# Packed output projection and moved edge work in a gated attention and expert kernel

## The chip, the cores and the metric

The kernel runs on one core of a Trainium2 chip. Its engines work side by side, each in its own order: TensorE (PE, with its weight loads as PEld), VectorE (DVE), ScalarE (ACT), GpSimd (POOL) and SyncE (SP, which here only issues DMAs). ACT and POOL issue DMAs too. The metric is the time of one execution on the device in microseconds (us). Lower is better.

## What is computed

x has 2048 rows of 448 numbers in float32. Two branches read it, and a gate mixes them:

```python
x = A_x
g = _sigmoid((x * gate_w).sum(-1, keepdims=True))
a = _A_ref(x, A_wqkv, A_wo)
b = _B_ref(x, B_w_gate, B_w1, B_w2)
return g * a + (1 - g) * b
```

Branch a is attention with 16 heads of 28 numbers: softmax(q k^T / sqrt(28)) v for each head, the heads side by side, times wo (448 x 448). Branch b is a mixture of 8 experts: each row goes to the two experts with the largest of 8 logits x @ w_gate, each expert is silu(x @ w1[e]) @ w2[e] with 1792 hidden numbers, and the two results are added with softmax weights of the two logits.

## The kernel before

Most products are made from float32 numbers split in two: a high part h (rounded to the type float32r) and a low part l = value - h. A product is then h*h + h*l + l*h, three matmuls. A 448-row operand is held as four blocks of 128 partitions. The fourth has only 64 rows, so those rows stand in it twice: the upper 64 partitions take the low part (`split_xl`, L162), so that block needs two matmuls, not three. That makes 11 matmuls for a full product.

The stages, in PE's order:

1. **Front and v projection** (L251 to L391). x comes in 16 tiles of 128 rows on SP. `wv_r` holds the v columns of wqkv, and behind them the columns of wgate (D to D + E) and of gate_w (one column): one product gives v, the logits and the gate. `rows4` (L208) loads a 448-row operand in three DMAs: rows 0 to 383, and rows 384 to 447 twice. ACT splits `wv_r` block by block (L351), DVE makes the low parts (L335), and PE does 11 matmuls for a tile (L369). Before that, PE turns identity matrices (`busy`).
2. **q and k projection** (L561 to L617): `qk_tile` does four groups of 11 matmuls (L572), each into one of four PSUM banks `pq`; ACT copies the high part out (`hi`, L581), DVE the low part (`lo`, L584), and SP stores both to DRAM. Between the matmuls (at two places of a group, `A_AT`) `route(5)` issues up to five steps of the generator `routing` (L400); a step that yields a true value ends the call. Its last steps build, for four pairs of halves, one-hot masks `ob` and `ot` on DVE (L495, L499), products of `ot` on POOL and ACT (L502, L504), and then matmuls that turn them into lists of row numbers (L515). The last `qk_tile` also transposes the first expert's five x tiles in its groups (`first_x`, L599; `x_tile`, L227).
3. **Experts** (L785 to L896). For each expert, two halves of 7 hidden tiles: 22 matmuls for a hidden tile (L818) in two accumulators, silu on ACT (L820 to L826), the high part of a w2 block on ACT (L726, called at L823) and its low part on POOL (L732, called at L829), w1's split for the tiles ahead, and the low part of the hidden numbers on POOL (L741). Then five row tiles times w2 (L862 for the short tile k = 4, L868 for the others; the order is 4, 0, 1, 2, 3, counted by n_k). Between these, `worked` fits in matmuls of the row maxima of the scores (L106), which DVE reduces (L125) and SP stores (L144). An expert has room for 576 rows; rows beyond are done by `spilled` (L744), a loop over a count known only at run time. It is entered in the last expert, within the fourth row tile (n_k = 3, k = 2), ahead of f = 3.
4. **Attention** (L970 to L1041). A unit is one of four groups of four heads (g) and one of four quarters of the queries (qc), so there are 16 units (u = 4g + qc), with 16 key tiles (kt) each. Scores run three key tiles ahead of the products with v, which gather in one PSUM bank `po` (L1003). At a unit's end DVE copies `po` to `osb` (L1007) and POOL sends the row sums through DRAM to all partitions (`spread_sums`, L956). In the next unit `divide` (L964) multiplies by the reciprocal, one quarter at each of kt = 6 to 9, into `OT`. `OT`, `wo_h` and `wo_l` hold one 128-partition block for each head group: four heads of 28 rows at partitions 0, 32, 64 and 96, the rest unused. `beside` (L1011) also issues K and V loads, and in the last head group the gathers of the experts' rows (`fetch_routed`, L919, two indirect DMAs on POOL) and their weighted sum (`routed`, L928, two DVE operations).
5. **Output projection** (L1043 to L1051). For each of 16 tiles: `project` (L946), 12 matmuls (three for each of the four blocks) into one of four PSUM banks in turn; `split_o` of the tile four ahead (ACT L939, DVE L943; four buffers); `finish` (L951), which adds the gated sums on DVE and stores the tile on SP. The last unit is divided a quarter at a time behind tiles 3 to 6.

The order on PE, DVE and ACT is the program's in stages 1 and 2; in the experts POOL's too; in attention and after it only PE's and DVE's. The other engines' instructions, SP's always, are placed by the framework's scheduler at compile time.

## Time and profile before

| | us |
|---|---|
| median of 3 runs | 1485.94 |
| lowest and highest of them | 1484.88 and 1489.9 |
| profiled execution | 1484.16 |
| its span, first to last instruction | 1482.4 |
| front and v projection | 0 to 53 |
| q and k projection | 53 to 132.3 |
| experts | 132.3 to 946.6 |
| attention | 946.6 to 1439.3 |
| output projection | 1439.3 to 1482.4 |

The bounds of the stages are the starts of their first matmuls in the trace. A row of the timeline names start, length, engine, line, operation, what is written and read, and a count; the bracket gives the engine's idle time before it and what ended that. A row of the waits names the waiting engine, tile and line, then what it waited for, then the total in us, how often, and the longest. A row of the chain of work that ended last gives start, length and what. A row of the busy times by stage gives the stretch, its length, the busy time of each engine with its number of instructions, the clock that TensorE was granted (1.00 is full), the mean busy share of the DMA engines, and GB/s.

### The profile page before, as it was taken

How to read it: one execution, taken by the hardware profiler on the slowest of the kernel's cores; microseconds unless marked ns; L12 is line 12 of the kernel's file. 1: busy time of each engine (PE TensorE's matmuls, PEld its weight loads, DVE VectorE, ACT ScalarE, POOL GpSimd, SP SyncE). 2: the span in 40 equal slices, each digit the busy share in tenths (PEclk: the TensorE clock that was granted, in tenths of full speed). 3: DMA queues.
4: the chain of work that ended last, by engine and by line, in shares of the span. 5: the costliest groups of instructions: out<-in, count | busy, mean ns of one | idle time of the engine just before them, and what ended most of it. 6: DMA issues, size and time to landing. Idle time of an engine off the chain costs nothing.

```text
span 1482.4 us, 28384 instructions
## 1 busy us (share of the span) xinstructions
PE 1460.7 (99%) x11380; PEld 980.4 (66%) x11380; DVE 786.5 (53%) x680; ACT 902.9 (61%) x1579; POOL 657.5 (44%) x707
## 2 busy tenths in 40 slices
PE   8999999999999999999999999799999999999998
PEld 7878888888878888888788888433333333333348
DVE  4645767767767767777777778011123111223245
ACT  5334355344444543543444434499999999999981
POOL 2123587587566765874775656211122111124330
PEclk9999999999999999999999999999999999999999
DMA  9777631343133323323431320300221221143212
GB/s 323 259 265 226 178 96 55 107 130 117 62 108 115 89 90 110 103 68 99 129 118 39 107 61 4 89 21 22 77 66 44 61 63 33 29 120 98 74 42 99
DMA packets 107958, 147.97 MB, mean 100 GB/s; under 512 B 17356, under 2 KB 83308, under 8 KB 107824
## 3 DMA queue, kind: packets, MB, share of 16 engines
q1 hardware_dynamic: 98192, 124.90, 27.3%
q0 software_dynamic: 9344, 20.78, 4.7%
q8 instruction: 90, 1.47, 0.4%
q10 hardware_dynamic: 288, 0.46, 0.1%
q14 instruction: 44, 0.36, 0.1%
HBM read 108.56 MB, written 37.51 MB: 99 GB/s over the span
## 4 chain that ended last, share of the span: by engine, by line
PE 95%; issue 1%; DVE 1%; ACT 1%; DMA 1%; POOL 0%; SPq 0%; POOLq 0%; ACTq 0%
PE acc L818 23%; PE acc L868 19%; PE po L1003 17%; PE ps L991 16%; PE pm L106 6%; PE pq L572 4%; PE acc L862 3%; PE pq L369 2%; PE ps L949 2%; PE acc L106 2%; PE acc L714 1%; PE po L949 1%; PE pt L331 0%; DMA wv_r<-in_gate_w_dram 0%; DVE ot L499 0%
## 5 line engine op out<-in xcount | busy, mean ns | idle before, releaser
L125 DVE TENSOR_REDUCE mp<-pm 128x6 f32<-128x3072 f32 (+1 forms) x164 | 542.0, 3306 | 121.3 <-PE pm L106 121.3
L994 ACT ACTIVATE P<-ps 128x1536 f32<-128x1536 f32 x256 | 371.4, 1451 | 0.2
L1003 PE MATMUL po<-P,V 128*32 128x512 f32 x2048 | 272.8, 604 | 0.0
L818 PE MATMUL acc<-xeh,w1l 128*128 128x288 f32 x880 | 259.4, 302 | 0.0
L818 PE MATMUL acc<-xeh,w1h 128*128 128x288 f32 x880 | 256.0, 298 | 0.0
L991 PEld LDWEIGHTS ps<-Q,Kh 29*128 29x128 f32 (+1 forms) x2048 | 78.8, 183 | 217.7 <-ACT P L993 212.4
L732 POOL TENSOR_TENSOR w2l<-w2r,w2h 128x448 fp32r<-128x448 f32 x112 | 129.3, 1154 | 198.4 <-ACT w2h L726 198.4
L991 PE MATMUL ps<-Q,Kh 29*128 29x512 f32 (+1 forms) x2048 | 191.4, 444 | 3.7 <-ACT P L993 3.6
L818 PE MATMUL acc<-xel,w1h 128*128 128x288 f32 x660 | 194.8, 295 | 0.0
L958 POOL DMA_DIRECT2D sum_d<-osb x64 | 32.0, 510 | 347.0 <-DVE osb L1007 323.3
L820 ACT ACTIVATE hh<-acc 128x288 fp32r<-128x288 f32 x224 | 92.5, 413 | 148.3 <-PE acc L818 148.1
L818 PEld LDWEIGHTS acc<-xeh,w1l 128*128 128x128 f32 x880 | 165.9, 189 | 21.7 <-issue 21.5
L868 PE MATMUL acc<-w2h,hh 128*128 128x448 f32 x448 | 173.7, 388 | 4.9 <-DMA Kh<-qkh_d 4.9
L818 PEld LDWEIGHTS acc<-xeh,w1h 128*128 128x128 f32 x880 | 165.8, 188 | 7.6 <-issue 7.3
L868 PE MATMUL acc<-w2h,hl 128*128 128x448 f32 x448 | 169.1, 378 | 0.0
L1007 DVE COPY osb<-po 128x512 f32<-128x512 f32 x16 | 11.1, 692 | 293.6 <-PE po L1003 243.6
L868 PE MATMUL acc<-w2l,hh 128*128 128x448 f32 x448 | 164.4, 367 | 0.0
L993 ACT ACTIVATE P<-ps 128x512 f32<-128x512 f32 x256 | 153.5, 600 | 3.5 <-PE ps L991 2.3
L694 POOL TENSOR_TENSOR w1l<-w1r,w1h 128x512 fp32r<-128x512 f32 (+1 forms) x88 | 137.8, 1566 | 18.9 <-ACT w1h L688 6.7
L741 POOL TENSOR_TENSOR hl<-hf,hh 128x512 fp32r<-128x512 f32 x112 | 143.5, 1288 | 0.0
L818 PEld LDWEIGHTS acc<-xel,w1h 128*128 128x128 f32 x660 | 124.6, 189 | 1.7 <-issue 1.5
L106 PE MATMUL pm<-khg,qg 28*128 28x512 f32 x969 | 118.2, 454 | 0.4 <-DVE mp L125 0.4
(183 smaller groups left out, 1963.0 us busy)
## 6 DMA issues: line engine op xcount, KB each, us to landing
w2r<-in_B_w_dram SPq DMA_DIRECT2D x112, 224.0 KB
w1r<-in_B_w_dram SPq DMA_DIRECT2D x56, 384.0 KB
w1r<-in_B_w_dram SPq DMA_DIRECT2D x112, 64.0 KB
qkh_d<-hi SPq DMA_DIRECT2D x28, 256.0 KB
qkl_d<-lo SPq DMA_DIRECT2D x28, 256.0 KB
ys_d<-yo SPq DMA_DIRECT2D x32, 224.0 KB
ys_d<-zf SPq DMA_DIRECT2D x24, 224.0 KB
v_d<-v_s SPq DMA_DIRECT2D x16, 256.0 KB
```

The costliest lines, as they stand in the source:

```text
L106: nc.tensor.matmul(banks[n], qgs[g, qt // 4][rw, (qt % 4) * 128:(qt % 4 + 1) * 128], kh[g, kc][rw], start=True, stop=True)
L125: nc.vector.tensor_reduce(mp[:, (o + lo) % 256:(o + lo) % 256 + hi - lo], pm[:, lo:hi], axis=AX.X, op=ALU.max)
L694: nc.gpsimd.tensor_tensor(l[:, :, half], r[:, :, half], h[:, :, half].bitcast(F32), op=ALU.subtract)
L732: nc.gpsimd.tensor_tensor(w2l, w2r, w2h.bitcast(F32), op=ALU.subtract)
L741: nc.gpsimd.tensor_tensor(hl, hf32, hh[:, 0:512].bitcast(F32), op=ALU.subtract)
L818: nc.tensor.matmul(pu[:, 0:HC], a, b[:, cs], start=i == 0, stop=i == len(mms) - 1)
L820: nc.scalar.activation(hh[:, cs], pu[:, 0:HC], AF.Silu)
L868: nc.tensor.matmul(py[:n, 0:w], a[:, cs], b, start=i == 0, stop=i == 3 * NH - 1)
L991: nc.tensor.matmul(p3[:, j - 1] if j else p1, k[rw, ks], qs[u][rw, c], start=i == 0, stop=i == 2)
L993: nc.scalar.activation(P[:, 0], p1, AF.Exp, scale=SCALE)
L994: nc.scalar.activation(P[:, 1:4], p3, AF.Exp, scale=SCALE)
L1003: nc.tensor.matmul(po[32 * j:32 * j + 32], v[:, kt % 8, 32 * j:32 * j + 32], P[:, j], start=kt == 0, stop=kt == NT - 1)
```

## The change

- **Front**: wgate's rows 0 to 383 are loaded on ACT's queue, between the two wv blocks there, and its last rows, twice, on SP's, after wv's last and ahead of x tile 2. Before, all three were on POOL's queue ahead of gate_w's last rows.
- **Routing**: the step that makes `ob` now ends its call of `route`; one of the pauses behind the pairs is gone.
- **First x tiles**: they are transposed two, two, one, none in the groups of the last `qk_tile`; before: two, one, one, one.
- **w2**: in the first half of the first expert, w2's blocks are split one hidden tile later; the last hidden tile there splits two.
- **Overflow loop**: it is entered ahead of f = 6, the last one of the row tile, and not of f = 3.
- **Output projection**: `wo` and `OT` are packed as the other 448-row operands are, in four blocks of 128 with the last 64 rows twice, so a tile takes 11 matmuls. `divide` works in place on `osb`; once its last quarter is done, SP copies each head's rows to their place in `OT`, in pieces where a head crosses a block's edge, and twice for rows from 384 on. The last unit's four quarters are all divided behind tile 3.
- **Gathers**: each unit u fetches tile u at kt = 1 and sums it at kt = 12.

```diff
@@ -254,8 +254,9 @@
         nc.gpsimd.memset(warm, 0.0)
         load_x(0)
         load_x(1)
-        for b in range(2):
-            nc.scalar.dma_start(wv_r[:, b, 0:D], wqkv[b * 128:(b + 1) * 128, 2 * D:3 * D])
+        nc.scalar.dma_start(wv_r[:, 0, 0:D], wqkv[0:128, 2 * D:3 * D])
+        rows4(wv_r[:, :, D:D + E], wgate, nc.scalar, slice(0, 1))
+        nc.scalar.dma_start(wv_r[:, 1, 0:D], wqkv[128:256, 2 * D:3 * D])
         nc.scalar.activation(warm[:, 1:2], warm[:, 0:1], AF.Copy)
         nc.sync.dma_start(wv_r[:, 2, 0:D], wqkv[256:384, 2 * D:3 * D])
         for b in range(2):
@@ -264,8 +265,8 @@
         nc.gpsimd.iota(jp, pattern=[[1, 128]], base=0, channel_multiplier=-1,
                        allow_small_or_imprecise_dtypes=True)
         nc.vector.tensor_scalar(ident, jp, 0.0, None, op0=ALU.is_equal)
-        rows4(wv_r[:, :, D:D + E], wgate, nc.gpsimd)
         rows4(wv_r[:, :, D + E:D + E + 1], gw.unsqueeze(1), nc.gpsimd, slice(1, 3))
+        rows4(wv_r[:, :, D:D + E], wgate, nc.sync, slice(1, 3))
         nc.gpsimd.memset(wv_r[:, :, NV - 1], 0.0)
         for t in range(2, NXT - 1):
             load_x(t)
@@ -494,7 +495,7 @@
                     ob = wk.tile([128, 8, 128], BF, name="xt", bufs=NXT)
                     nc.vector.tensor_tensor(ob, bc(iob.unsqueeze(1), [128, 8, 128]),
                                             bc(bb[:, c, hs_].unsqueeze(2), [128, 8, 128]), op=ALU.is_equal)
-                    yield
+                    yield "pause"
                     ot = sb.tile([128, 8, NTL], BF, name="ot", bufs=2)
                     nc.vector.tensor_tensor(ot, bc(iob[:, 0:NTL].unsqueeze(1), [128, 8, NTL]),
                                             bc(tb[:, c, hs_].unsqueeze(2), [128, 8, NTL]), op=ALU.is_equal)
@@ -504,7 +505,6 @@
                     nc.scalar.mul(mv[:, :, 1], ot, iop)
                     pairs.append((ob, mv))
                     yield "pause"
-            yield "pause"
             yield "pause"
             yield "pause"
             yield "pause"
@@ -597,7 +597,7 @@
         xe = []
 
         def first_x(c):
-            for k in ((0, 1), (2,), (3,), (4,))[c]:
+            for k in ((0, 1), (2, 3), (4,), ())[c]:
                 x_tile(xgs[k], k, lambda: ps.tile([128, 4, 128], F32, name="pt"), *xe)
 
         next(ms)
@@ -798,6 +798,8 @@
                     p = e * NP + ft // 2
                     i2 = e * NF + ft
 
+                    w2_now = [i2] if e or hf else [i2 - 1, i2][f == 0:1 + (f == NH - 1)]
+
                     ahead = p + 1 if 2 <= ft < 6 or ft >= 8 and ft < 12 or e == 0 and ft < 2 else None
                     w1h, w1l = w1t[p][1:]
                     fs = HALVES[ft % 2]
@@ -820,13 +822,15 @@
                         nc.scalar.activation(hh[:, cs], pu[:, 0:HC], AF.Silu)
                         if c == 0:
                             nc.scalar.activation(hf32[:, 0:HC], pu[:, 0:HC], AF.Silu)
-                            split_w2_high(i2)
+                            for i in w2_now:
+                                split_w2_high(i)
                         else:
                             nc.scalar.activation(hf32[:, HC:512], pu[:, 0:512 - HC], AF.Silu)
                             nc.scalar.activation(ht, pu[:, 512 - HC:HC], AF.Silu)
                             if ahead:
                                 split_w1_high(ahead, HALVES[ft % 2])
-                    split_w2_low(i2)
+                    for i in w2_now:
+                        split_w2_low(i)
                     if ahead:
                         split_w1_low(ahead, HALVES[ft % 2])
                     if lag:
@@ -854,7 +858,7 @@
                     for f in range(NH):
                         hh, hl, ht = hs[f]
                         w2h, w2l, w2r = w2t[base + f]
-                        if (e, hf, n_k, f) == (E - 1, 1, 3, 3):
+                        if (e, hf, n_k, f) == (E - 1, 1, 3, NH - 1):
                             assert not flush and next(ms, 0) == 0
                             spilled()
                         if k == 4:
@@ -903,18 +907,20 @@
     v1[1] = load_v(0, 1)
     sb = ctx.enter_context(tc.tile_pool(name="pc_sb", bufs=2, reuse_waits="tile"))
     ps = ctx.enter_context(tc.tile_pool(name="pc_ps", bufs=1, space=PSUM, reuse_waits="tile"))
-    wo_h = sb.tile([128, NG, D], F32R, name="wo_h", bufs=1)
-    wo_l = sb.tile([128, NG, D], F32R, name="wo_l", bufs=1)
-    OT = sb.tile([128, NG, S], F32, name="OT", bufs=1)
-
-    def split_wo(g):
-        w_ = sb.tile([128, D], F32, name="yg0")
-        nc.gpsimd.memset(w_, 0.0)
-        for j in range(4):
-            r0 = (4 * g + j) * DH
-            nc.gpsimd.dma_start(w_[32 * j:32 * j + DH], wo[r0:r0 + DH])
-        nc.vector.tensor_copy(wo_h[:, g], w_)
-        nc.vector.tensor_tensor(wo_l[:, g], w_, wo_h[:, g].bitcast(F32), op=ALU.subtract)
+
+    wo_h = sb.tile([128, 4, D], F32R, name="wo_h", bufs=1)
+    wo_l = sb.tile([128, 4, D], F32R, name="wo_l", bufs=1)
+    OT = sb.tile([128, 4, S], F32, name="OT", bufs=1)
+
+    def split_wo(b):
+        w_ = sb.tile([128, D], F32, name="wo_r")
+        if b < 3:
+            nc.gpsimd.dma_start(w_, wo[b * 128:(b + 1) * 128])
+        else:
+            nc.gpsimd.dma_start(w_[0:64], wo[384:448])
+            nc.gpsimd.dma_start(w_[64:128], wo[384:448])
+        nc.vector.tensor_copy(wo_h[:, b], w_)
+        nc.vector.tensor_tensor(wo_l[:, b], w_, wo_h[:, b].bitcast(F32), op=ALU.subtract)
 
     def fetch_routed(t):
         yg = []
@@ -934,19 +940,22 @@
 
     def split_o(t, eng):
         ts = slice(t * 128, (t + 1) * 128)
-        oh = sb.tile([128, NG, 128], F32R, name="oh", bufs=4)
+        oh = sb.tile([128, 4, 128], F32R, name="oh", bufs=4)
         if eng is nc.scalar:
             nc.scalar.activation(oh, OT[:, :, ts], AF.Copy)
         else:
             nc.vector.tensor_copy(oh, OT[:, :, ts])
-        ol = sb.tile([128, NG, 128], F32R, name="ol", bufs=4)
-        nc.vector.tensor_tensor(ol, OT[:, :, ts], oh.bitcast(F32), op=ALU.subtract)
+        ol = sb.tile([128, 3, 128], F32R, name="ol", bufs=4)
+        split_xl(OT[:, :, ts], oh, ol, 128)
         halves[t] = (oh, ol)
 
     def project(pa_, oh, ol):
-        for g in range(NG):
-            for i, (a, b) in enumerate(((oh, wo_h), (oh, wo_l), (ol, wo_h))):
-                nc.tensor.matmul(pa_, a[:, g], b[:, g], start=g == 0 and i == 0, stop=g == NG - 1 and i == 2)
+        mms = []
+        for j in range(3):
+            mms += [(oh[:, j], wo_h[:, j]), (oh[:, j], wo_l[:, j]), (ol[:, j], wo_h[:, j])]
+        mms += [(oh[:, 3], wo_h[:, 3]), (oh[:, 3], wo_l[:, 3])]
+        for i, (a, b) in enumerate(mms):
+            nc.tensor.matmul(pa_, a, b, start=i == 0, stop=i == len(mms) - 1)
 
     def finish(t, pa_, b1):
         nc.vector.scalar_tensor_tensor(b1, pa_, coef[:, 0, t:t + 1], b1, op0=ALU.mult, op1=ALU.add)
@@ -964,8 +973,22 @@
     def divide(g, qc, k, osb, rs):
         cs = slice(k * 128, (k + 1) * 128)
         nc.vector.reciprocal(rs[:, cs], rs[:, cs])
-        nc.vector.tensor_tensor(OT[:, g, qc * 512 + k * 128:qc * 512 + (k + 1) * 128], osb[:, cs],
-                                rs[:, cs], op=ALU.mult)
+        nc.vector.tensor_tensor(osb[:, cs], osb[:, cs], rs[:, cs], op=ALU.mult)
+        if k < 3:
+            return
+
+        qs_ = slice(qc * 512, (qc + 1) * 512)
+        for j in range(4):
+            r = (4 * g + j) * DH
+            end = r + DH
+            p = 32 * j
+            while r < end:
+                n = min(end, (r // 128 + 1) * 128) - r
+                for twice in range(2 if r >= 384 else 1):
+                    o = r % 128 + 64 * twice
+                    nc.sync.dma_start(OT[o:o + n, r // 128, qs_], osb[p:p + n])
+                r += n
+                p += n
 
     ctx.enter_context(tc.manual_schedule(engines={mybir.EngineType.PE, mybir.EngineType.DVE}))
     todo = []
@@ -1024,11 +1047,10 @@
             held[g][1][1] = load_v(g, 1)
         if g == 1 and qc == 1 and kt % 4 == 1:
             split_wo(kt // 4)
-        if g == NG - 1 and kt in (1, 4, 7, 10):
-            fetch_routed(4 * qc + kt // 3)
-        if g == NG - 1 and kt in (3, 6, 12, 14):
-            t = 4 * qc + {3: 0, 6: 1, 12: 2, 14: 3}[kt]
-            b1s[t] = routed(t)
+        if kt == 1:
+            fetch_routed(u)
+        if kt == 12:
+            b1s[u] = routed(u)
         if u == 4 * NG - 1 and kt in (2, 5, 11, 13):
             split_o({2: 0, 5: 1, 11: 2, 13: 3}[kt], nc.vector)
 
@@ -1046,8 +1068,9 @@
         project(pa_, *halves.pop(t))
         if t + 4 < NT:
             split_o(t + 4, nc.scalar)
-        if 3 <= t < 7:
-            divide(NG - 1, 3, t - 3, *ended[4 * NG - 1])
+        if t == 3:
+            for k in range(4):
+                divide(NG - 1, 3, k, *ended[4 * NG - 1])
         finish(t, pa_, b1s.pop(t))
```

## The prediction

> **What bounds the kernel now.** I read the page first, then the busy times by stage, then the waits of TensorE over the whole span, and only then the places that those waits name.
>
> ```profile
> span 1482.4 us, 28384 instructions
> PE 1460.7 (99%) x11380; PEld 980.4 (66%) x11380; DVE 786.5 (53%) x680; ACT 902.9 (61%) x1579; POOL 657.5 (44%) x707
> ```
>
> ```profile
> 0.00:53.00 53.00, 48.20 (x256) 43.09 (x257) 23.78 (x60) 26.13 (x61) 11.68 (x59) 1.00 0.93 320
> 53.00:132.30 79.30, 75.59 (x378) 61.36 (x377) 42.17 (x101) 25.27 (x48) 13.77 (x11) 1.00 0.72 245
> 132.30:946.60 814.30, 808.69 (x5440) 669.90 (x5440) 591.53 (x300) 355.98 (x944) 524.12 (x456) 1.00 0.32 96
> 946.60:1439.30 492.70, 488.97 (x5121) 170.06 (x5120) 105.72 (x183) 487.89 (x514) 103.91 (x173) 1.00 0.22 60
> 1439.30:1482.40 43.10, 39.19 (x195) 35.98 (x192) 23.32 (x37) 7.61 (x12) 4.02 (x8) 0.99 0.26 92
> ```
>
> The columns after a window's length are the busy times of PE, PEld, DVE, ACT and POOL. The stages are: v projection and routing logits; q and k projections; experts; attention; output projection. In every one PE is busy nearly throughout. So the time falls in two ways only: PE gets fewer matmuls, or one of its few pauses goes. The pauses, longest first:
>
> ```profile
> PE acc L868 <- DMA Kh<-qkh_d: 4.9, 1, 4.9
> ...
> PE pq L572 <- DVE lo L584: 2.3, 1, 2.3
> PE acc L818 <- DVE xeh L164: 1.4, 1, 1.4
> ...
> PE acc L818 <- ACT ht L826: 0.3, 1, 0.3
> ```
>
> Each row gives total, count and longest. The rows L868, L572 and the two L818 are pauses that this change works on; so is a late start for lack of data, which this list shows only in pieces.
>
> **Part 1, the front.** The first x tile is projected when all four row blocks of wv_r, with the columns of wgate and gw, have landed.
>
> ```profile
> 2.55 1.90 POOL L211 DMA_DIRECT2D wv_r<-in_B_w_gate_dram  x3
> ...
> 4.42 1.07 POOL L211 DMA_DIRECT2D wv_r<-in_gate_w_dram  x2
> 7.91 1.54 ACT L351 ACTIVATE xeh<-wv_r 128x458 fp32r<-128x458 f32 x3 [1.72 <-DMA wv_r<-in_B_w_gate_dram]
> 10.23 0.59 ACT L351 ACTIVATE xeh<-wv_r 128x458 fp32r<-128x458 f32 x1 [0.78 <-DMA wv_r<-in_gate_w_dram]
> 11.54 0.48 PE L369 MATMUL pq<-xel,xh 128*128 128x458 f32 x1 [0.17 <-DVE xel L335]
> ```
>
> The reader is to see one queue: POOL issues three wgate pieces and only then the last two of gw, whose landing at 10.23 us releases the last split; PE goes on at 11.54. With wgate on ACT's and SP's queues, POOL issues gw 1.9 us sooner (the three issues' 1.90 us). The same landing delay then puts the split at about 8.3 us, and ACT, whose first three splits take 1.54 us, is ready by then if the wgate piece lands before 6.9 us. It is issued at about 1.2 us on ACT, behind one block of wv. On SP the two wgate pieces delay the x loads by two issues, about 1.1 us as POOL's two at 4.42; only tile 2's could matter, which is needed after the last split. I take 1.8 us. Bounds: 0, if the many small pieces on ACT's queue hold up wv's second block by as much; 2.5, if gw isn't last any more (7.91 + 1.54 - 1.72 = 7.7 us in place of 10.23).
>
> **Part 2, routing.** The reader is to see a chain that goes round between DVE and ACT, in program order on both.
>
> ```profile
> 72.34 0.69 DVE L584 TENSOR_TENSOR lo<-pq,hi 128x512 fp32r<-128x512 f32 x1 [1.28 <-ACT hi L581]
> 72.94 1.22 DVE L495 TENSOR_TENSOR xt<-iob,bb 128x1024 bf16<-128x1024 bf16 x1
> 74.08 0.69 DVE L499 TENSOR_TENSOR ot<-iob,tb 128x512 bf16<-128x512 bf16 x1
> ...
> 78.62 1.89 DVE L584 TENSOR_TENSOR lo<-pq,hi 128x512 fp32r<-128x512 f32 x3 [1.27 <-ACT hi L581]
> ```
>
> ```profile
> 71.09 0.72 ACT L504 ACTIVATE xt<-ot,iop 128x512 bf16<-128x512 bf16 x1 [1.86 <-DVE ot L499]
> 71.72 0.58 ACT L581 ACTIVATE hi<-pq 128x512 fp32r<-128x512 f32 x1
> 74.80 0.72 ACT L504 ACTIVATE xt<-ot,iop 128x512 bf16<-128x512 bf16 x1 [2.49 <-DVE ot L499]
> ```
>
> ```profile
> 84.13 37.05 PE pq L572 x163
> ```
>
> A PSUM bank pq is free after `hi` on ACT and `lo` on DVE. ACT's `hi` stands behind L504, which waits for `ot`. One group of 11 matmuls takes PE 11 x 37.05/163 = 2.50 us. Two pairs of masks per group make the round 78.62 - 72.34 = 6.28 us, in two groups: 7.6 us behind PE. The pause was 2.3, so the four banks absorb 5.3. With the added pause a group has one pair: lo to ob 0.60, ob to ot 1.14, ot to L504 0.72, L504 to hi 0.63, hi to lo 0.62, so 3.71 us in four groups: 4 x 1.21 = 4.8 us behind, within 5.3. I take 2.0 of the 2.3 us. Bounds: 2.3, and -1: three more calls of `route` come later, and an `ot` slowed beside POOL would lengthen the round. The index matmuls move three calls (3.8 us) later, before gathers that are used only 30 us on.
>
> **Part 3, start of the experts.** Tile 4 of x is split one group earlier, so its DVE work isn't last before the first L818: 1.4 us gone. ACT no longer meets this row in the first hidden tile:
>
> ```profile
> 136.77 0.58 ACT L726 ACTIVATE w2h<-w2r 128x448 fp32r<-128x448 f32 x1 [2.03 <-DMA w2r<-in_B_w_dram]
> ```
>
> The silu behind it came late and PE paused 0.3 us. One tile (over 2.9 us of PE) later w2 is there; the last tile's second split has the k = 4 products to hide behind. Sum 1.7 us; bounds 0.3 (if the last group's `lo` is as late for a PSUM bank as tile 4 was) and 1.7.
>
> **Part 4, the overflow loop.** No instruction of the loop's body is in the trace (nothing overflows), but entering the loop joins all engines.
>
> ```profile
> 932.15 0.37 PE L868 MATMUL acc<-w2h,hl 128*128 128x448 f32 x1
> ```
>
> ```profile
> 932.94 3.32 DMA m_d<-mr
> ...
> 937.46 9.18 PE acc L868 x33
> ...
> 1449.30 7.30 PE ps L949 x36
> ```
>
> ```profile
> 78.00:79.00 1.00, 0.00 (x0) 0.00 (x0) 0.38 (x1) 1.00 (x4) 0.52 (x1) 1.00 0.00 0
> ...
> 935.00:936.00 1.00, 0.00 (x0) 0.00 (x0) 0.00 (x0) 0.00 (x0) 0.00 (x0) 0.66 0.01 1
> ...
> 942.00:943.00 1.00, 1.00 (x6) 0.88 (x6) 0.00 (x0) 0.55 (x1) 0.05 (x1) 0.93 0.00 0
> ```
>
> PE ends at 932.52 and goes on at 937.46. Who is late is in the chain: the store of the last maxima, issued at 932.94, lands at 936.27, and SP waits for it before the join. (The wait list blames a Kh load, which stands behind the join.) Its transpose stands ahead of f = 3 and doesn't move. So moving the loop from f = 3 to f = 6 gives PE nine matmuls, 9 x 7.30/36 = 1.8 us, inside the wait; the pause falls to 3.1 us. Besides, the clock (last but two of the columns) fell to half from about 935.3 (a mean of 0.66 in that slice) and came back at 942.1: 33 matmuls took 9.18 us where 33 x 0.203 = 6.7 do at full clock. If it doesn't fall, the 24 matmuls left take 4.9 in place of 9.18: 4.3 us in all. Bounds: 0, if PE's own way into the loop is the limit and all comes later with it; 4.3.
>
> Does the clock fall after 3.1 us? At 78 us a pause of 2.3 left it at 1.00; here it fell 2.8 us after the last matmul, but not before. [...]
>
> **Part 5, attention.** The gathers (two a unit, L923) and L931, L932 move from the last four units to one tile a unit, at kt = 1 and 12; OT is filled by 4 to 8 SP copies a unit (22 for each quarter of the queries, 88 in all).
>
> ```profile
> 1012.44 0.69 DVE L1007 COPY osb<-po 128x512 f32<-128x512 f32 x1 [18.48 <-PE po L1003]
> 1021.03 0.95 DVE L966 RECIPROCAL rs<-rs 128x128 f32<-128x128 f32 x1 [7.90 <-DMA rs<-sum_d]
> ```
>
> A unit is 492.70/16 = 30.8 us. The copies wait for the four divisions, which start 8.6 us after the unit's end and take about 5; behind the waiting copies SP holds the loads of Q, K and V, which are a unit or half a unit early, so even 8 copies of 0.5 us are hidden. A gather's POOL time lies behind the sums of the unit before, some 8 us in; the DVE work that needs it comes at 12/16 of 30.8 = 23 us, and DVE is busy 106 of 493 us. Cost 0; without that cover each unit would pay (third rival). PE work is the same, wo's fewer loads are hidden too.
>
> **Part 6, output projection.**
>
> ```profile
> 1449.81 0.69 DVE L943 TENSOR_TENSOR ol<-OT,oh 128x512 fp32r<-128x512 f32 x1 [1.15 <-ACT oh L939]
> 1450.41 0.95 DVE L966 RECIPROCAL rs<-rs 128x128 f32<-128x128 f32 x1
> 1451.39 0.29 DVE L967 TENSOR_TENSOR OT<-osb,rs 128x128 f32<-128x128 f32 x1
> 1451.60 0.68 DVE L952 SCALAR_TENSOR_TENSOR b<-po,coef,b 128x448 f32<-128x448 f32 x1
> ```
>
> Eleven matmuls replace twelve in 16 tiles: 16 x 0.203 = 3.2 us, all on the path (PE has no gap there). A tile then takes 2.23 us. What is late next: the four divisions stand together ahead of tile 3's `finish`, 4 x (1451.60 - 1450.41) = 4.8 us. By DVE's order, counted from the stage's start: tile 7's `ol` is done near 10.5, the divisions at 15.3, `finish(3)` at 16.0. Project 7 wants that PSUM bank at 7 x 2.23 = 15.6: a pause of 0.4 us. After that DVE needs about 1.5 us a tile of 2.23 and catches up. The eight copies go out from 15.3 to about 19 and land by 22; tile 12's split comes after project 8 at 20.5 and its product at 27, so some 3.5 us are to spare after the split's 1.5. I take 2.8 us. Bounds: 3.2, and 1 if copies and divisions are each 2 us slower.
>
> **Sum.** 1.8 + 2.0 + 1.7 + 4.3 + 0 + 2.8 = 12.6 us. The profiled execution took 1484.16 us, span 1482.4; so 1471.6 by it. The three runs' median, 1485.94, is 1.8 above it and would give 1473.3. I forecast 1472.5 us. A difference under 0.3% (4.5 us) can't be told from no change. With the lower ends (0 - 1 + 0.3 + 0 + 0 + 1) the kernel stays as it is; all of them together is unlikely, the upper ends give 14 us.
>
> **Rivals.**
>
> 1. *The clock falls again in the shorter pause.* For: it fell 2.8 us after the last matmul. [...] Then part 4 is 1.8 and not 4.3: 1475.
> 2. *PE's loop entry is its own limit, and a late datum takes the front's place.* Part 4 is 0, and 1.8 of part 1 goes, because the DMA engines are busy 0.93 of the first 53 us (first window row, next to last column) and the small pieces now stand ahead of wv. 1472.5 + 4.3 + 1.8 = 1478.6. Against: PE has nothing to load there but one register, and SP's wait is in the chain.
> 3. *The end of each unit pauses PE* (slower). One PSUM bank `po` serves all units: the next unit's first product waits for L1007, and that stands on DVE behind L931, which now waits in every unit for a gather on POOL. For: DVE goes in order, and POOL's order isn't written by hand in this stage. If a gather lands past kt = 15, that is over 25 us after its place, PE pays from there on; at 2 us in 15 units 30 us, 1472.5 + 30 = 1502.5. It beats the gain from 0.8 us a unit. Against: 23 us of cover.
> 4. *The change doesn't do what it says*: the added pause spaces the masks, but `ot` beside POOL and three later calls give the pause back elsewhere (part 2 at -1, part 3 at 0.3): 1472.5 + 4.4 = 1476.9.
>
> **How the numbers follow.** Forecast as it stands 0.50; rival 1 0.20; rival 2 0.08; rival 4 0.08; rival 3 0.06; several small losses together, so that less than 4.5 us is left, 0.08. Faster by over 0.3% (below 1481.5) are the forecast and rivals 1, 2 and 4: 0.86; within 0.3%: 0.08; slower: 0.06. The range 1468.5 to 1480 holds the first four cases: below by 1.4 us more than the upper ends' 1470 for a quick run, above rival 2 with 1.4 us to spare. It leaves out 0.14.
>
> **What would show it.** Front: L351's last split near 8.3 us and not 10.23. Routing: the PE row L572 <- DVE lo gone or under 0.5. Experts: both small L818 rows gone. Loop: a PE pause of about 3.1 us at L868, and no slice with a clock below 0.9 around it; a slice of 0.5 shows rival 1. Attention: the first to the last L1003 as far apart as before; a row po L1003 <- DVE osb shows rival 3. End: 176 matmuls at L949's place in place of 192, and one pause below 1 us near tile 7. I am wrong if PE's busy time falls by more than these 16 matmuls and the slow-clock stretch, or if a pause shows up at a place that isn't named here.

## The result, and the profile after

The changed kernel takes 1473.52 us (median of 6 runs, 1471.49 to 1474.54), the kernel before in the same session 1486.42 us. The ratio is 0.9908, with a 95% interval from 0.9894 to 0.9921. The profiled execution took 1474.54 us with a span of 1472.7 us, 9.7 us less than the span before.

First the page of the changed kernel, then its busy times by stage (columns as before).

```profile
span 1472.7 us, 28497 instructions
PE 1457.8 (99%) x11364; PEld 976.8 (66%) x11364; DVE 788.5 (54%) x696; ACT 902.5 (61%) x1579; POOL 650.0 (44%) x689
```

```profile
0.00:52.30 52.30, 47.53 (x256) 42.56 (x257) 23.69 (x60) 26.01 (x61) 9.87 (x56) 1.00 0.93 316
52.30:127.60 75.30, 75.27 (x378) 61.56 (x377) 40.71 (x100) 24.45 (x47) 12.06 (x11) 1.00 0.75 258
127.60:937.80 810.20, 807.53 (x5438) 669.24 (x5437) 591.63 (x300) 356.33 (x945) 524.11 (x456) 1.00 0.31 97
937.80:1431.90 494.10, 490.83 (x5121) 170.51 (x5120) 106.56 (x187) 488.23 (x514) 100.02 (x158) 0.99 0.24 68
1431.90:1472.70 40.80, 36.61 (x179) 32.89 (x176) 25.88 (x49) 7.49 (x12) 3.93 (x8) 1.00 0.31 106
```

Read the second number of each row, the stage's length, against the same row of before. Four stages are shorter: by 0.7, 4.0, 4.1 and, the last, 2.3 us. Attention is longer by 1.4. (The first matmul of a stage bounds it; one record may be missing at the start of the experts, so that bound is good to some 0.2 us.) 0.7 + 4.0 + 4.1 - 1.4 + 2.3 = 9.7.

The waits of TensorE in the changed kernel, longest first:

```profile
PE ps L1014 <- ACT P L1016: 3.0, 3, 1.6
PE pq L341 <- DVE ident L267: 2.9, 1, 2.9
PE acc L872 <- DMA Kh<-neg_d: 2.3, 1, 2.3
PE pq L370 <- ACT xeh L352: 1.1, 1, 1.1
PE po L958 <- DVE b L961: 0.5, 1, 0.5
```

Of the rows that the change worked on, the one in q and k (2.3) and the two at the start of the experts (1.4 and 0.3) are gone. The loop's row fell from 4.9 to 2.3. A row of 0.5 us in the output projection is new, at the place and nearly of the size that part 6 gave. No row has `po` waiting for `osb`: rival 3 didn't come.

The front, in the timeline of the changed kernel:

```profile
1.15 0.45 ACTq L211 DMA_DIRECT2D wv_r<-in_B_w_gate_dram  x1
...
7.66 2.02 ACT L352 ACTIVATE xeh<-wv_r 128x458 fp32r<-128x458 f32 x4 [1.40 <-DMA wv_r<-in_B_w_gate_dram]
```

All four splits run in one go here, so in this execution gw holds up nothing any more. But the first of them begins at 7.66 us, hardly ahead of the 7.91 of before, because wgate's first piece lands only then, 6.5 us after its issue.

The loop, in the chain of work that ended last:

```profile
927.80 1.94 DMA m_d<-mr
...
931.23 6.65 PE acc L872 x24
```

The last row is the one to see: 24 matmuls took 6.65 us, where 24 at full clock take 4.9 (0.203 each, from 36 in 7.30 us before). The first of them are long in the timeline, too, and the clock comes back at 934.4:

```profile
931.23 0.74 PE L872 MATMUL acc<-w2h,hh 128*128 128x448 f32 x1 [2.32 <-DMA Kh<-neg_d]
931.77 0.57 PE L872 MATMUL acc<-w2l,hh 128*128 128x448 f32 x1
...
934.38 0.40 PE L872 MATMUL acc<-w2h,hl 128*128 128x448 f32 x1
...
942.24 1.23 PE L1014 MATMUL ps<-Q,Kh 29*128 29x512 f32 x8 [0.85 <-ACT P L1016]
...
948.86 0.74 PE L1014 MATMUL ps<-Q,Kh 29*128 29x512 f32 x8
```

The last two rows lie in the begin of attention (first score at 937.80): a group of eight score matmuls took 1.23 us at 942 and 0.74 at 949, when the clock was back. The busy times there, in the changed kernel:

```profile
943.00:946.00 3.00, 3.00 (x24) 0.69 (x20) 0.00 (x0) 2.47 (x3) 2.29 (x3) 0.50 0.85 199
946.00:949.00 3.00, 2.86 (x24) 0.87 (x24) 0.49 (x1) 0.71 (x2) 2.49 (x3) 0.65 1.08 352
```

And for the whole first unit, from its first score to the first copy of `po`, in the kernel before and in the changed kernel:

```profile
946.56:982.01 35.45, 32.69 (x349) 11.80 (x352) 0.00 (x0) 34.82 (x38) 8.00 (x13) 1.00 0.30 74
```

```profile
937.80:975.85 38.05, 35.37 (x349) 12.58 (x352) 1.18 (x3) 35.02 (x38) 8.08 (x9) 0.91 0.32 98
```

The clock column (last but two) says it: 0.50 and 0.65 in the two slices, and 0.91 over the unit against 1.00 before. The first unit took 38.05 us, against 35.45 before. So 2.6 us were lost in the first 12 us of attention, and the other units gave 1.2 of it back. The fourth busy time is ACT's. It is nearly the same in both (34.82 and 35.02 us), so ACT is busy for nearly all of the unit before, and 2.4 of the 2.6 us are time in which ACT stands idle: 38.05 - 35.02 = 3.0 us, against 0.6.

### The profile page after: what moved, and what is told of

Same layout as the page of the kernel before. It is cut to its first block, busy times and chain, and to the rows that moved or that the text cites. A ratio compares the mean times of both kernels' runs of the same rounds, so it can differ in the third digit from the quotient of the medians.

```text
span 1472.7 us, 28497 instructions
## 1 busy us (share of the span) xinstructions
PE 1457.8 (99%) x11364; PEld 976.8 (66%) x11364; DVE 788.5 (54%) x696; ACT 902.5 (61%) x1579; POOL 650.0 (44%) x689
## 4 chain that ended last, share of the span: by engine, by line
PE 97%; issue 1%; ACT 1%; DMA 1%; DVE 1%; POOL 0%; SPq 0%; POOLq 0%; another core or an unknown queue 0%; DVEq 0%; ACTq 0%
PE acc L820 23%; PE acc L872 19%; PE po L1026 17%; PE ps L1014 16%; PE pm L106 6%; PE pq L572 5%; PE acc L866 3%; PE pq L370 2%; PE acc L106 2%; PE ps L958 1%; PE acc L714 1%; PE po L958 1%; PE pt L332 0%; DVE rs L975 0%; DMA wv_r<-in_A_wqkv_dram 0%
```

## The experiments

Theory A is the prediction's working as the profile after corrects it: each part is worth what its own stage shows, and the parts don't meddle with each other. The rivals (theory B) differ by run and stand in its expectation. For the reading, one table: where q and k began, where attention began, the length of its first unit, and the time from the first matmul of the output projection to the span's end, each from the run's own profile.

| kernel | median us | ratio to before, interval | q, k at | attention at | first unit | projection |
|---|---|---|---|---|---|---|
| before | 1486.42 | | 52.97 | 946.56 | 35.45 | 43.09 |
| rep_before | one run, 1484.09 | | 52.97 | 946.08 | 36.68 | 43.06 |
| changed | 1473.52 | 0.9908, 0.9894 to 0.9921 | 52.26 | 937.80 | 38.05 | 40.77 |
| u_front | 1474.55 | 0.9924, 0.9900 to 0.9948 | 52.93 | 938.57 | 37.71 | 40.59 |
| u_route | 1476.18 | 0.9935, 0.9911 to 0.9959 | 51.67 | 939.85 | 37.73 | 40.36 |
| u_first | 1474.21 | 0.9922, 0.9897 to 0.9947 | 52.04 | 937.64 | 37.73 | 40.39 |
| u_loop | 1476.72 | 0.9933, 0.9909 to 0.9958 | 52.68 | 942.08 | 37.59 | 40.74 |
| u_gather | 1475.40 | 0.9929, 0.9912 to 0.9945 | 52.95 | 938.75 | 37.98 | 40.77 |
| u_pack | 1475.33 | 0.9926, 0.9910 to 0.9943 | 52.01 | 937.64 | 37.57 | 42.92 |
| t_finish | 1473.15 | 0.9914, 0.9898 to 0.9931 | 52.51 | 938.36 | 37.28 | 39.98 |
| p_exp | 1472.27 | 0.9907, 0.9890 to 0.9923 | 51.93 | 935.92 | 39.02 | 40.60 |
| f_gate_first | 1473.81 | 0.9922, 0.9905 to 0.9938 | 51.62 | 935.86 | 37.97 | 40.39 |
| l_late | 1472.09 | 0.9908, 0.9892 to 0.9925 | 51.47 | 935.69 | 38.10 | 40.39 |
| best | 1472.99 | 0.9910, 0.9896 to 0.9924 | 51.45 | 936.91 | 38.00 | 39.69 |

The intervals overlap, so single edits of 1 or 2 us aren't told apart by the whole time; the rows of their own stage tell them apart. Still, the medians add up: with one part undone at a time (the six u_ kernels) they stand 1.0, 2.7, 0.7, 3.2, 1.9 and 1.8 above the changed kernel's, together 11.3 of the 12.9 between the medians. That is a hint and no proof, since each of these differences is as small as the spread of single executions. The move of w2 has no run of its own.

### u_front: the front as before

```diff
-        nc.scalar.dma_start(wv_r[:, 0, 0:D], wqkv[0:128, 2 * D:3 * D])
-        rows4(wv_r[:, :, D:D + E], wgate, nc.scalar, slice(0, 1))
-        nc.scalar.dma_start(wv_r[:, 1, 0:D], wqkv[128:256, 2 * D:3 * D])
+        for b in range(2):
+            nc.scalar.dma_start(wv_r[:, b, 0:D], wqkv[b * 128:(b + 1) * 128, 2 * D:3 * D])
...
+        rows4(wv_r[:, :, D:D + E], wgate, nc.gpsimd)
         rows4(wv_r[:, :, D + E:D + E + 1], gw.unsqueeze(1), nc.gpsimd, slice(1, 3))
-        rows4(wv_r[:, :, D:D + E], wgate, nc.sync, slice(1, 3))
```

> The changed kernel with the old order of the front loads alone. In the changed kernel q and k's first matmul starts at 52.26 us, before at 52.97. Theory A (the new front is worth the 0.7 us seen there and no more, because wgate's piece still lands as late as before): the start goes back to 52.9 to 53.0 and the time rises by 0.7 us. Theory B (the front brought 1.8 us, of which something else in the change ate 1.1): the start goes to 54.0, the time rises by 1.8 us.

q and k begin at 52.93 us, 0.67 later than in the changed kernel and where they began before. In the timeline of u_front the last split is released by gw again:

```profile
10.21 0.59 ACT L351 ACTIVATE xeh<-wv_r 128x458 fp32r<-128x458 f32 x1 [0.79 <-DMA wv_r<-in_gate_w_dram]
```

The front is worth 0.7 us in this pair. Among the nine profiles that have the new front as it is, q and k begin anywhere from 51.47 to 52.95 us, so the part is worth 0 to 1.5 us from one execution to the next.

### u_route: the pauses of routing as before

```diff
-                    yield "pause"
+                    yield
                     ot = sb.tile([128, 8, NTL], BF, name="ot", bufs=2)
...
+            yield "pause"
             yield "pause"
```

> The changed kernel with the old pauses in routing alone. Theory A (the round between DVE and ACT made the pause): a PE row L572 <- DVE lo of 2.3 us comes back, and the stretch from q and k's first matmul to the experts' first grows from 75.4 to about 77.7 us. Theory B (the pause went for another reason, such as the earlier start or fewer DMAs on POOL): no such row, the stretch stays within 0.3 us.

The row of before comes back in the waits of u_route, and the q and k stage is 129.65 - 51.67 = 77.98 us long, 2.6 more than the 75.36 of the changed kernel:

```profile
PE pq L573 <- DVE lo L585: 2.3, 1, 2.3
```

### u_first: the first x tiles as before

```diff
-            for k in ((0, 1), (2, 3), (4,), ())[c]:
+            for k in ((0, 1), (2,), (3,), (4,))[c]:
```

> The changed kernel with the first x tiles transposed two, one, one, one as before. Theory A (tile 4's DVE work is last): PE waits 1.4 us for DVE at the first matmul of the experts, the stretch from q and k to the experts grows by 1.3 to 1.4 us. Theory B (the first matmul waits for a PSUM bank of the last group in any case): no wait, within 0.3 us.

The waits of u_first have the old row, and its stage is 1.4 us longer (76.75). Its chain shows something else, which no theory had named:

```profile
PE acc L820 <- DVE xeh L164: 1.4, 1, 1.4
```

```profile
932.49 5.23 PE acc L872 x24
```

Behind a pause of 2.28 us at the loop, all but the same as in the changed kernel, the 24 matmuls took 5.23 us (in the last row) and not 6.65: here the clock didn't fall. One thing that differs is where the pause lies. In the changed kernel half clock begins and ends at 931.03 and 934.44, and at 941.27 and 948.09, so these times are 3.41 us or twice that apart. The busy times in stretches of 3.41 us: the two of the changed kernel behind which its clock falls, at the loop and in attention, and then the two at the pause in u_first, counted back from its fall at 941.11:

```profile
927.62:931.03 3.41, 1.29 (x7) 0.85 (x5) 0.00 (x0) 0.00 (x0) 0.00 (x0) 1.00 0.23 82
...
937.85:941.27 3.42, 1.79 (x25) 0.94 (x24) 0.00 (x0) 3.34 (x4) 1.13 (x1) 1.00 0.22 75
```

```profile
927.46:930.87 3.41, 2.75 (x15) 2.22 (x13) 0.28 (x1) 0.00 (x0) 0.86 (x1) 1.00 0.21 75
930.87:934.28 3.41, 1.79 (x9) 1.65 (x10) 0.00 (x0) 0.55 (x1) 0.25 (x1) 1.00 0.15 42
```

In the changed kernel nearly the whole pause lies in one stretch, in which TensorE is busy for 1.29 us of 3.41, and the clock falls at its end. In u_first the pause is split over two, with 2.75 and 1.79 us busy, and the clock stays at 1.00. So it does in p_exp and f_gate_first; in the other seven profiles with a pause of 2.3 us there it falls. That the place of the pause decides isn't shown: 1.79 us busy stands once ahead of a fall and once not.

### u_loop: the loop ahead of f = 3 again

```diff
-                        if (e, hf, n_k, f) == (E - 1, 1, 3, NH - 1):
+                        if (e, hf, n_k, f) == (E - 1, 1, 3, 3):
```

> The changed kernel with the loop ahead of f = 3 again. In the changed kernel PE pauses 2.32 us and 24 matmuls take 6.57 us behind it. Theory A (SP's wait for the last stores sets when all go on): the pause is 2.32 + 9 x 0.206 = 4.2 us, 33 matmuls follow in 8.4 to 9.2 us, according to where the half clock starts and ends, so that PE is 1 to 3 us later at the attention's start. Theory B (PE's own way into the loop sets it): the pause stays at 2.3 us, and PE is at the attention's start at the same time.

The experts stage is 814.03 us, 3.85 more than in the changed kernel. The store of the maxima and the matmuls behind the loop, in the chain of u_loop:

```profile
928.45 3.11 DMA m_d<-mr
...
932.46 9.70 PE acc L872 x33
```

TensorE's pause is 4.7 us here, against 2.3 in the changed kernel, and the clock stays low for 6.8 us and not 3.4. SP waits 1.5 us for the store here and 0.3 in the changed kernel. It comes to that wait 1.6 us after the store's issue in both, so these two figures show only when the store landed: 3.11 us after its issue, and 1.94. In the three profiles with the loop ahead of f = 3 the landing took 3.1 to 3.4 us, in the ten with it ahead of f = 6 of the same row tile 1.7 to 2.0; why isn't shown. So of the 2.4 us between the pauses about half is the landing, and the rest is the matmuls that now run inside the wait. The move does what part 4 says, and the shorter landing comes with it.

### l_late: the loop one row tile later still

```diff
-                        if (e, hf, n_k, f) == (E - 1, 1, 3, NH - 1):
+                        if (e, hf, n_k, f) == (E - 1, 1, 4, NH - 1):
```

> The changed kernel with the loop entered ahead of f = 6 of the last row tile (n_k = 4) in place of the fourth: 21 more matmuls, 4.3 us, inside the wait. Theory A (what is late at the loop is the store of the last maxima, landing 1.9 us after its issue): it has landed long before, so the row at the loop falls from 2.3 us to under 1, the clock stays full behind it, and only three matmuls stand between the loop and attention, so that a K load behind the join may hold the first scores by up to 1 us; the experts stage is 1 to 2.5 us shorter than 810.2, in all 1471.5 us. Theory B (the join has a cost of its own on PE and on SP, whatever has landed): the pause stays at 2 us or more and the K loads behind it come later than the first scores want them; the stage is 810 to 813 us, in all 1473.5 to 1476 us.

SP's wait, the semaphore instructions of the loop's line on TensorE's own queue, PEldq (count, shortest, median and longest in ns, starts of the first and the last), and the timeline around the loop in l_late:

```profile
SPq L748 <- PEq L748: 0.5, 1, 0.5
```

```profile
L748 PEldq EVENT_SEMAPHORE  x14: 51/51/51, 932.7 to 934.5; - x14
```

```profile
927.32 1.08 SPq L144 DMA_DIRECT2D m_d<-mr  x1
...
932.32 0.37 PE L872 MATMUL acc<-w2h,hl 128*128 128x448 f32 x1
...
934.88 0.48 PE L872 MATMUL acc<-w2h,hh 128*128 128x448 f32 x1 [2.19 <-DMA Kh<-neg_d]
```

The store was issued 5 us ahead of TensorE's last matmul, and now it is SP that waits for TensorE at the join. Yet the pause is 2.19 us. That is theory B for the pause: with the store landed, entering the loop still costs TensorE 2.2 us, and its own queue works through 14 semaphore instructions in that time, from 932.7 to 934.5 us, 0.14 us apart in the mean. The stage is shorter by 1.3 us (808.86), since the clock now falls at 936.0, behind the stage's last matmul; but attention begins with it (half clock from 936.0 to 946.2 us), and its first unit is as long as elsewhere. As a whole nothing is won that the interval could show.

### u_gather: the gathers in the last four units again

```diff
-        if kt == 1:
-            fetch_routed(u)
-        if kt == 12:
-            b1s[u] = routed(u)
+        if g == NG - 1 and kt in (1, 4, 7, 10):
+            fetch_routed(4 * qc + kt // 3)
+        if g == NG - 1 and kt in (3, 6, 12, 14):
+            t = 4 * qc + {3: 0, 6: 1, 12: 2, 14: 3}[kt]
+            b1s[t] = routed(t)
```

> The changed kernel with the gathers and their sums back in the last four units. From the first unit's end to the last unit's end the attention took 457.4 us before and 456.2 with the change; before, the two intervals between unit ends that stand out were 31.0 and 31.2 us, both in the last head group. Theory A (gathers and sums crowded into the last units made those two long): they come back, about 1.2 us. Theory B (they were chance, or came from the loads for the old OT): every interval stays at 30.4 to 30.7 us but for one.

The copies of `po` at the ends of the last units, in the timelines of u_gather and of the changed kernel:

```profile
1374.96 0.69 DVE L1030 COPY osb<-po 128x512 f32<-128x512 f32 x1 [16.65 <-DMA Q<-m_d]
...
1406.81 0.69 DVE L1030 COPY osb<-po 128x512 f32<-128x512 f32 x1 [16.21 <-PE po L1026]
```

```profile
1372.80 0.69 DVE L1030 COPY osb<-po 128x512 f32<-128x512 f32 x1 [17.66 <-DMA Q<-m_d]
...
1403.22 0.69 DVE L1030 COPY osb<-po 128x512 f32<-128x512 f32 x1 [17.55 <-PE po L1026]
```

A unit of 31.85 us against 30.42. From first to last copy it is 458.93 against 456.21: the spread gathers are worth 2.7 us here, more than the 1.2 by which the two first profiles differ. But the kernel before, whose gathers stand in the last four units too, took 457.42 and 456.61 us in its two profiles, so they are worth 0.4 to 2.7 us. The first unit is 37.98 us also without a gather in it, so the gathers aren't what slows it.

### u_pack: wo and OT as before

```diff
-    wo_h = sb.tile([128, 4, D], F32R, name="wo_h", bufs=1)
+    wo_h = sb.tile([128, NG, D], F32R, name="wo_h", bufs=1)
...
-        nc.vector.tensor_tensor(osb[:, cs], osb[:, cs], rs[:, cs], op=ALU.mult)
...
-                    nc.sync.dma_start(OT[o:o + n, r // 128, qs_], osb[p:p + n])
+        nc.vector.tensor_tensor(OT[:, g, qc * 512 + k * 128:qc * 512 + (k + 1) * 128], osb[:, cs],
+                                rs[:, cs], op=ALU.mult)
```

`split_wo`, `split_o` and `project` are those of before, too; the four divisions stay together behind tile 3.

> The changed kernel with the old layout of wo and OT: 12 matmuls a tile, divisions written straight into OT, no copies on SP; the divisions still stand together behind tile 3. Theory A (the packing is worth the 16 matmuls and nothing else; the slower first unit of attention is the clock's doing, not the packing's): the output projection takes 40.8 + 16 x 0.205 = 44.0 us up to the span's end, the pause near tile 7 stays, and the first unit of attention is again 37 to 39 us long if a slice of it shows the clock near half, 35 to 36 if none does; 1476.5 us in all. Theory B (the new tiles or the copies slow the ramp of attention): the first unit is back at 35.5 us whatever the clock, so that the whole is 1474 us although the projection is longer.

The projection takes 42.92 us, 2.15 more than in the changed kernel and 1.1 less than I had said. In the chain of u_pack TensorE never stops, and 36 matmuls take what they took before:

```profile
1440.98 7.30 PE ps L954 x36
1448.29 2.43 PE po L954 x12
```

The pause, which I had expected to stay, is gone: a tile of 12 matmuls takes 2.43 us, so project 7 comes 1.4 us later and meets a bank that is free. The first unit of attention is again 37.57 us: theory B falls, the packing isn't what slows it.

### t_finish: tile 3 finished ahead of the divisions

```diff
+        finish(t, pa_, b1s.pop(t))
         if t == 3:
             for k in range(4):
                 divide(NG - 1, 3, k, *ended[4 * NG - 1])
-        finish(t, pa_, b1s.pop(t))
```

> The changed kernel with tile 3's finish ahead of the four divisions. In the changed kernel the projection runs 37.8 us from its first matmul to the end of its last one, with a pause of 0.5 us ahead of project 7 and matmuls 0.207 us apart behind it, 0.203 ahead of it. Theory A (the divisions ahead of finish made the pause, and the pause the wider spacing): no pause, 0.203 throughout, the stage 0.8 to 0.9 us shorter. Theory B (the copies into OT, which take 6 us, are the next to be late): the pause goes, but PE waits for tile 12 instead, or the spacing still widens.

The projection takes 39.98 us, 0.8 less. The chain of t_finish, and then that of the changed kernel around project 7:

```profile
1440.81 6.69 PE ps L958 x33
...
1449.72 6.84 PE ps L958 x33
```

```profile
1447.51 0.69 DVE b L961
...
1448.34 2.51 PE po L958 x11
1450.84 6.82 PE ps L958 x33
```

In the changed kernel the chain passes from DVE's `b` to TensorE: that is the pause, and it goes with this edit, as theory A has it. 33 matmuls in 6.69 us are 0.203 us each, in 6.82 or 6.84 they are 0.207. I had put that widening down to the pause; here it comes without one, so that half of theory A falls.

### p_exp: a small Exp right behind the loop

```diff
                             spilled()
+                            nc.scalar.activation(warm_e, ident[:, 0:2], AF.Exp)
```

> The changed kernel with one small Exp on ACT right behind the overflow loop, so that the table for the attention is loaded while ACT is idle. In five profiles of the change and its variants the first unit takes 37.6 to 38.1 us and the clock falls to half for 6.8 us from 3.1 to 3.5 us after the attention's first matmul; before, it took 35.5 us and the clock stayed. Theory A (the gaps of PE while ACT loads the table are what the clock gate acts on): the table load of 1.28 us is gone from the start, the gaps are shorter, the clock stays full, and the first unit takes about 34 us: 3 to 4 us less. Theory B (the fall is due to something else there, such as the loop's pause before it): the clock falls as before and only 1.3 us goes.

ACT loads its table while it idles (1.28 us, from 929.90), and the clock stays at 1.00 at the loop, but the first unit is 39.02 us, the longest of all. The busy times of p_exp around 950 us:

```profile
947.00:950.00 3.00, 1.58 (x20) 0.66 (x20) 0.69 (x1) 2.23 (x3) 0.44 (x2) 0.99 0.61 205
950.00:953.00 3.00, 3.00 (x20) 1.04 (x20) 0.00 (x0) 2.18 (x4) 1.29 (x2) 0.50 0.48 154
```

The clock is at half here, after a first fall about 940, and at 947 to 950 both TensorE and ACT (first and fourth busy time) stand for part of the time. The 3 to 4 us that theory A promised aren't there; what the early table load gave was lost again. Nor is it shown that the gaps bring the fall.

### f_gate_first: wgate ahead of wv's block on ACT's queue

```diff
-        nc.scalar.dma_start(wv_r[:, 0, 0:D], wqkv[0:128, 2 * D:3 * D])
         rows4(wv_r[:, :, D:D + E], wgate, nc.scalar, slice(0, 1))
+        nc.scalar.dma_start(wv_r[:, 0, 0:D], wqkv[0:128, 2 * D:3 * D])
```

> The changed kernel with wgate's large piece first on ACT's queue, ahead of wv's first block. In four profiles of the changed front ACT's first split starts at 7.0 to 8.1 us, mostly on wgate's landing, though its piece is issued at 1.15 us. Theory A (the piece waits in the queue behind wv's 224 KB block): it lands 1 us or more sooner, the first split starts at 6.2 to 6.5 us. Theory B (its 384 small pieces, mixed with the other queue's large ones, take that long wherever they stand): the first split stays at 7 us or later, and wv's blocks may land later still.

```profile
0.73 0.46 ACTq L211 DMA_DIRECT2D wv_r<-in_B_w_gate_dram  x1
...
6.52 1.79 ACT L352 ACTIVATE xeh<-wv_r 128x458 fp32r<-128x458 f32 x3 [0.33 <-DMA wv_r<-in_gate_w_dram]
8.85 0.59 ACT L352 ACTIVATE xeh<-wv_r 128x458 fp32r<-128x458 f32 x1 [0.55 <-DMA wv_r<-in_B_w_gate_dram]
```

In the timeline of f_gate_first the piece is issued 0.4 us sooner and the first split begins 1.1 us sooner than in the profile after. That doesn't show that the piece had waited behind the block of wv. In the nine profiles with the order of the changed kernel the first split begins at 6.83 to 8.35 us, and in six of them, as here, it is a piece of gw that it waits for; 6.52 here and 6.77 in best lie just below them. The last split waits for wgate's rows on SP now. The front begins q and k at 51.62 us, within the range of the nine.

### rep_before: the kernel before, profiled again

> The kernel before, unchanged, for a second profile. Theory A (the fall of the clock in the first unit of attention goes by the phase of a free-running window): the first unit, from the first score to the first copy of po, is 35.5 us if no slice of its first 15 us has the clock below 0.9, and 37 to 39 if one has; either can come. Theory B (something in the changed kernel brings the fall): 35.5 us and a full clock again. In both the pause at the overflow loop is 4.7 to 5.0 us, the clock near half for some 3.4 to 7 us behind it, and the output projection 43 us.

The first unit is 36.68 us long, neither 35.5 nor 37 to 39. The busy times of rep_before there:

```profile
951.00:954.00 3.00, 3.00 (x28) 0.95 (x24) 0.00 (x0) 2.65 (x3) 2.70 (x5) 0.60 0.97 212
954.00:957.00 3.00, 3.00 (x32) 0.98 (x32) 0.00 (x0) 2.01 (x3) 1.12 (x2) 0.83 1.14 271
```

A fall of the clock for some 3.4 us is in it: (1 - 0.60) x 3 + (1 - 0.83) x 3 = 1.7 us of full clock are missing, which is 3.4 us at half. So the kernel before has the fall too, in one of two profiles, and 1.2 of the 2.6 us can come and go without any change. That the fall goes by a window's phase, as theory A has it, isn't shown.

### best: t_finish and f_gate_first together

```diff
-        nc.scalar.dma_start(wv_r[:, 0, 0:D], wqkv[0:128, 2 * D:3 * D])
         rows4(wv_r[:, :, D:D + E], wgate, nc.scalar, slice(0, 1))
+        nc.scalar.dma_start(wv_r[:, 0, 0:D], wqkv[0:128, 2 * D:3 * D])
...
+        finish(t, pa_, b1s.pop(t))
         if t == 3:
             for k in range(4):
                 divide(NG - 1, 3, k, *ended[4 * NG - 1])
-        finish(t, pa_, b1s.pop(t))
```

> The changed kernel with two edits that each did what it should alone: finish of tile 3 ahead of the last unit's divisions, and wgate's first piece ahead of wv's first block on ACT's queue. Theory A (they add up): q and k begin at 51.6 to 52.0 us, no pause of PE in the output projection, which takes 40.0 us to the span's end; 1472.4 us, ratio to the kernel before 0.990. Theory B (both are within what single executions differ by, through the clock's falls at the loop and in the first unit of attention): the two places look so in the profile, but the whole is 1473.5 us, ratio 0.9908 to 0.992.

Both places look as they should: q and k at 51.45, no pause in the projection, 39.69 us. The whole is 1472.99 us, 0.991 of the kernel before: not told apart from the changed kernel. TensorE's waits in best have a row that nobody releases, 1.2 us long, in the first unit of attention. The row, and the first unit's busy times in best:

```profile
PE ps L1014 <- issue: 1.2, 1, 1.2
```

```profile
936.91:974.91 38.00, 34.26 (x349) 12.20 (x352) 1.30 (x2) 35.01 (x38) 8.07 (x9) 0.96 0.32 97
```

The clock falls for half as long here as in the changed kernel (0.96 against 0.91 over the unit), and yet the unit is as long, with the same 3.0 us of ACT idle.

## Why the prediction held, and where it didn't

The time, 1473.52 us, is 1.0 above the forecast. The parts, by the prediction's numbers:

- **Part 1, 1.8 forecast, 0.7 measured (0.8 as the mean of the nine profiles).** The step that failed is the condition "if the wgate piece lands before 6.9 us", which I took as met. In the profile after, wgate's piece on ACT's queue landed at 7.7, and in two others of the nine with this front at 8.1 and 8.35. In the other six the first split began at 6.8 to 7.2, but in five of these the last one then waited for wgate's last rows on SP. In none was the last split near 8.3; it began at 8.7 us or later. Why the piece lands so late isn't shown (f_gate_first). Taking the nearest late datum away needed the bound of the next one as the likely value: 7.91 stood in the row of the three splits, which themselves had waited for wgate.
- **Part 2, 2.0 forecast, 2.6 by u_route.** Right: the whole pause is gone, and the three later calls gave nothing back: `ot` took 0.68 to 0.69 us all four times, where before it took 1.53 us twice, each time beside POOL's product. Rival 4 falls.
- **Part 3, 1.7 forecast, 1.4 by u_first and the row of 0.3 gone.** Right. w2's move wasn't undone alone; that the 0.3 is its doing is argued, not shown.
- **Part 4, 4.3 forecast, 3.3 measured.** From the 34th matmul ahead of attention, the last ahead of the loop before, to attention it is 946.56 - 932.15 = 14.41 us before and 937.80 - (928.55 - 9 x 0.203) = 11.08 after. The pause shrank by more than forecast, to 2.3 and not 3.1, because the store of the maxima landed in 1.94 us and not 3.32. The step that failed is "if it doesn't fall": the clock fell behind this shorter pause. That is rival 1, which I had priced at all of 2.5 us; the fall lasted 3.4 us and cost 1.4 to 1.8 (6.65 less u_first's 5.23, or less the 4.87 of full clock). That a pause of 3.1 us leaves the clock up was an estimate of mine that no run shows; behind the shorter pauses of 2.3 us at the loop it fell in seven of ten profiles. And rival 2's first half was nearer than I thought: I had held against it that TensorE has nothing to load there but one register, but l_late shows that its own way into the loop takes 2.2 us, so the move has given all that it can.
- **Part 5, 0 forecast, 1.4 lost.** The step covered the steady units only, and there it was too careful: the last units no longer pay for four tiles' gathers each (u_gather, 0.4 to 2.7). What it left out is the start of the stage, where TensorE and ACT wait for each other and the clock can fall. In the profile after, the matmuls between 941 and 948 are longer for it, and ACT stands 2.35 us for their scores. But the fall isn't all of the 2.6 us: with half of it the unit is as long in best and f_gate_first (38.00 and 37.97), and with 10.2 us of half clock it is no longer in l_late (38.10). What goes with the length is ACT's idle time in the unit: 0.6 us before, 1.6 in rep_before, 2.3 to 3.0 in the changed kernels, p_exp apart. That the first unit is 37.3 us or more in all twelve profiles of changed kernels and less in both of the kernel before isn't settled: gathers, packing, loop, front, routing and x tiles were each undone and none brought it back. In some of these profiles there is also a second stand of 1 to 2 us, as in best and p_exp, for which the profile names no cause. And two parts do meddle with each other: unit 5, in which wo is split, takes 30.8 to 31.05 us in the profiles with both the new gathers and the packing, and 30.43 in the others (before, rep_before, u_gather, u_pack).
- **Part 6, 2.8 forecast, 2.3 measured.** Right in its mechanism: u_pack and best differ by 42.92 - 39.69 = 3.2 us, the 16 matmuls, and the pause came at tile 7 with 0.5 where 0.4 was said. The rest is the wider spacing of matmuls behind it. The eight copies were hidden.

So the sum, 12.6, met 9.7 in the profile and 12.9 between the medians. The parts as measured add up to 9.2 (0.7 + 2.6 + 1.7 + 3.3 - 1.4 + 2.3); the 0.5 us left stand in the experts and have no cause shown. That the medians lie closer to the forecast than the profiled execution isn't a merit of the working: single executions of the kernel before lie up to 5 us apart (1484.88 to 1489.9), and two profiles can't show that spread.

## What to carry to other kernels

When a late datum is taken away, the gain ends at the next one: read what the instructions just before the stall waited for, and take that as the likely value. A pause can cost a second time if the clock falls behind it: the 2.3 us at the loop cost another 1.4 to 1.8 in the profile after, and in three of the ten profiles with that pause the clock stayed up; price it as a chance, and don't ask a single profile for it. To test whether a join is late for a datum or has a price of its own, move it so late that the datum must have landed.

## What the hardware showed beyond that

- **Half clock came behind stretches in which TensorE was busy for part of the time, and not behind others like them.** It stands from 935.31 to 942.14 us in the profile before, and from 931.03 to 934.44 and from 941.27 to 948.09 after: 6.83, 3.41 and 6.83 us. In the 3.41 us ahead of these three falls TensorE was busy for 0.62, 1.29 and 1.79 us. But in u_first full clock went on behind 1.79 us (930.87 to 934.28), and in the profile before behind 1.89 us (75.16 to 78.57) and 1.99 us (945.55 to 948.96). The busy times are the profile's, with matmul ends modelled and some records missing, so they are rough; what decides is open.
- **The loop over a run-time count, which runs zero times here,** cost TensorE 2.19 us at its entry in l_late, with the store landed.
- **A small load issued behind a large block on its queue** landed 6.5 us after its issue in the profile after, and some 6.9 and 7.2 us after it in u_loop and u_gather. Whether it lands sooner when it goes first, f_gate_first and best don't settle.
- **Matmuls of one shape** came 0.203 or 0.207 us apart at a granted clock of 1.00, the two in one execution (t_finish); what sets it is open.
